# Three row blocks on one ring, a scaling split around a root, and padding moved in TensorE's stream

## The chip, the cores and the metric

One core of one Trainium2 chip runs the whole program. The metric is the device time of one execution in microseconds (us), as a median of several runs; lower is better. A profiled execution lets the engines' instructions be read: TensorE (PE, with its weight loads as PEld), VectorE (DVE), ScalarE (ACT), GpSimd (POOL) and SyncE (SP), which here only issues DMAs.

## The reference

S = 2048 rows of width D = 640, H = 32 heads of size 128, the last W = 512 positions of a key and value cache, and a hidden width of F = 1728, all in fp32.

```
xn  = layernorm(x)                                  # over the last axis, eps 1e-5
q   = (xn @ wq) split into 32 heads of 128
p   = softmax(q k^T / sqrt(128)) over 512 positions # no mask
s   = concat(p v) @ wo                              # 2048 x 640
h   = relu(xn @ w1 + b1) ** 2                       # 2048 x 1728
out = x + s * silu(h @ w2 + b2)
```

## The kernel before

Rows are worked in four tiles of 512 (t = 0 to 3); everything is kept transposed, with the 640 features as 5 chunks of 128 partitions and the 512 rows along the free axis. Each fp32 operand is split into a high and a low part (`hi`, rounded by a ScalarE copy, and `lo`, the rest, by a subtraction on VectorE or GpSimd), and each product is the sum of three TensorE products, hi·hi, hi·lo and lo·hi.

The program has a first part, the MLP of tiles 0 to 2 in 42 steps (14 hidden chunks for each tile, `mlp_step(n)`: `up` of step n, then `down` of step n − 1), and a second, attention in 128 units (two halves, 16 groups of 2 heads, 2 tiles, 2 heads), with the rest of the MLP put in at its end. The order of instructions on each engine is the order in which they are written; in attention, a plan of due times sorts them.

The change lies mostly in `ln_first()`, the layernorm of tile 0, which nothing can run ahead of. Its 512 rows are four blocks of 128 rows, `xn[0]` to `xn[3]`, each 128 x 640. Block 0 comes in two halves, one by SP's DMA queue and one by ScalarE's; block 1 by SP's, block 2 by ScalarE's, block 3 by SP's. Meanwhile TensorE makes 40 transposes of the identity (`pw`) which nobody reads. Then:

- VectorE makes the statistics of a block (two `bn_stats`, one `bn_aggr`), block by block.
- Blocks 0 and 1 share one root: `root(0)` is a ScalarE square root, then a reciprocal on VectorE and a Newton step on GpSimd (`newton(0)`, four small instructions). ScalarE subtracts the mean (`centre`) and multiplies by the root (`scale`), 640 columns at a time; `scale(b)` also has TensorE transpose block b's five chunks (`turn`).
- Blocks 2 and 3 share the second: `root(1)` on ScalarE, between `scale(0)` and `scale(1)`, then the Newton step on VectorE, which also does subtraction and multiplication of both blocks, chunks 0 and 1 of block 2, the same of block 3, then chunks 2 to 4 of each.
- TensorE's transposes of chunk c of all four blocks gather in one PSUM bank, `px0_c`. ScalarE copies it into the high part of `xT`, VectorE makes the low part, and the first `up` starts.

`first_reads` puts the loads of the first weights on SP's queue behind a VectorE memset, so that they come after the x blocks. `ln_load(1)` then puts the next tile's four row blocks on SP's queue; each goes into the buffer of a block of tile 0 and waits until that has been transposed.

`pe.addr_align(BLOCK, slot)` inserts idle slots into TensorE's instruction stream until the next instruction stands at `slot` modulo 256. A matmul or transpose takes two slots (its weight load and itself), a separate wait takes one. In front of the warm-up there is one such alignment, to slot 88; in attention each unit has five (`align`, first at slot 188), which fix where the boundaries of 256 slots fall.

Of the kernel before, what the change touches and what calls it, by code (L numbers as in the profile page):

```python
# [10 lines left out]
AF = mybir.ActivationFunctionType  # L11
# [3 lines left out]
P = 128  # L15
NT = 512
EPS = 1e-5
WARM = 40
BLOCK = 256
FIRST_SLOT = 188  # L20
SLOTS = (0, 11, 22, 33, 42)
LEAD_SLOT = 88


@with_exitstack
def kernel(
# [19 lines left out]
    NB = NT // P  # L46
    DC = D // P
# [3 lines left out]
    LN_AT = {t: (3, 7) if t == LATE else (5, 9) for t in range(1, NTILE)}  # L51
# [12 lines left out]
    chunks = [(f0, min(P, F - f0)) for f0 in range(0, F, P)]  # L64
# [4 lines left out]
    class Ordered:  # L69
# [13 lines left out]
    pe, dve, act, pool, sp = (  # L83
        Ordered(e) for e in (nc.tensor, nc.vector, nc.scalar, nc.gpsimd, nc.sync)
    )
# [49 lines left out]
    def ln_tile(t, b):  # L135
        tag = "stage" if b < 2 else "mr"
        return xp.tile([P, D], F32, tag=tag, name=f"xb{t}_{b}")
# [88 lines left out]
    def ln_first():  # L226
        mv = xp.tile([P, 4, NB], F32, tag="mv", name="mv0")
        sc = xp.tile([P, 3, NB], F32, tag="sc", name="sc0")
        sts = [xp.tile([P, 2, 6], F32, tag="st", name=f"st0_{b}", bufs=4) for b in range(NB)]
        n = NB // 2  # L230
        M, R = ([mv[:, i, n * k : n * k + n] for k in range(2)] for i in range(2))
        VAR, SD, Y = ([sc[:, i, n * k : n * k + n] for k in range(2)] for i in range(3))
        warm = mv[:, 3, :1]
        pool.memset(warm, 1.0)
        eps = mv[:, 3, 1:2]
        dve.memset(eps, EPS)
        hd = D // 2
        xn = [ln_tile(0, b) for b in range(NB)]
        for i, q in enumerate((sp, act)):
            js = slice(i * hd, (i + 1) * hd)  # L240
            q.dma_start(xn[0][:, js], x[:P, js])
        for b in range(1, NB):
            (sp if b % 2 else act).dma_start(xn[b], x[b * P : (b + 1) * P, :])
        act.activation(warm, warm, AF.Sqrt)
        br = xp.tile([P, P], F32, tag="br", name="br", bufs=1)
        dve.memset(br, 0.0)
        BR.append(br)
        pw = psx.tile([P, NT], F32, tag="x", name="pw")
        pe.addr_align(BLOCK, LEAD_SLOT)
        for _ in range(WARM):  # L250
            pe.transpose(pw[:, :P], ident, ident)
        pts = [ps_y.tile([P, NT], F32, tag="py", name=f"px0_{c}") for c in range(DC)]
        xs = [
            xp.tile([P, DC, NT], F32R, tag=f"xT{i}", name=f"xT0_{i}", bufs=1) for i in range(2)
        ]

        def bn(b, i):
            dve.bn_stats(sts[b][:, i, :], xn[b][:, i * hd : (i + 1) * hd])

        def aggr(b):  # L260
            dve.bn_aggr(mv[:, :2, b], sts[b])

        def root(k):
            act.activation(SD[k], R[k], AF.Sqrt, bias=eps)
            dve.tensor_scalar(VAR[k], R[k], EPS, None, op0=ALU.add)

        def newton(k):
            if k == 0:
                pool.tensor_tensor(R[k], Y[k], Y[k], op=ALU.mult)
                pool.tensor_tensor(R[k], R[k], VAR[k], op=ALU.mult)  # L270
                pool.tensor_scalar(R[k], R[k], 0.5, -1.5, op0=ALU.mult, op1=ALU.add)
                pool.tensor_tensor(R[k], R[k], Y[k], op=ALU.mult)
            else:
                dve.scalar_tensor_tensor(R[k], Y[k], -0.5, Y[k], op0=ALU.mult, op1=ALU.mult)
                dve.tensor_tensor(R[k], R[k], VAR[k], op=ALU.mult)
                dve.scalar_tensor_tensor(R[k], R[k], 1.5, Y[k], op0=ALU.add, op1=ALU.mult)

        def centre(b):
            act.activation(xn[b], xn[b], AF.Identity, bias=mv[:, 0, b : b + 1], scale=-1.0)

        def scale(b):
            act.activation(xn[b], xn[b], AF.Identity, scale=R[0][:, b : b + 1])
            turn(b, range(DC))

        def turn(b, cs):
            for c in cs:
                pe.transpose(
                    pts[c][:, b * P : (b + 1) * P], xn[b][:, c * P : (c + 1) * P], ident
                )

        for b in range(n):
            for i in range(2):
                bn(b, i)
            aggr(b)
            if b == 0:
                raws = first_reads(br)
        centre(0)
        root(0)
        centre(1)
        bn(n, 0)  # L300
        dve.reciprocal(Y[0], SD[0])
        newton(0)
        bn(n, 1)
        aggr(n)
        for b in range(n + 1, NB):
            for i in range(2):
                bn(b, i)
            aggr(b)
        scale(0)
        root(1)  # L310
        scale(1)
        split_hi(0, raws[0], 0)
        dve.reciprocal(Y[1], SD[1])
        newton(1)
        for cs in (range(2), range(2, DC)):
            js = slice(cs[0] * P, (cs[-1] + 1) * P)
            for b in range(n, NB):
                m, q = mv[:, 0, b : b + 1], mv[:, 1, b : b + 1]
                dve.tensor_scalar(
                    xn[b][:, js], xn[b][:, js], m, q, op0=ALU.subtract, op1=ALU.mult  # L320
                )
            for c in cs:
                for b in range(n, NB):
                    turn(b, (c,))
        pool.tensor_copy(warm, xn[NB - 1][:, D - 1 :])
        split_lo(0, raws[0], 0, pool)
        for c in range(DC):
            act.activation(xs[0][:, c, :], pts[c], AF.Copy)
            dve.tensor_tensor(xs[1][:, c, :], pts[c], raw(xs[0][:, c, :]), op=ALU.subtract)
        split_hi(1, PRE[1, 0], 0)  # L330
        split_lo(1, PRE[1, 0], 0, pool)
        split_hi(0, raws[1], 1)
        split_lo(0, raws[1], 1, dve)
        return xs

    def spill(t, xs, cs=slice(0, DC)):
        for i in range(2):
            pool.dma_start(xT_d[t][i][:, cs, :], raw(xs[i])[:, cs, :])
# [25 lines left out]
    def split_hi(f, r, k):  # L364
        act.activation(split_parts(f, k)[0], r, AF.Copy)
# [92 lines left out]
    steps = [(t, f) for t in range(LATE) for f in range(FC)]  # L458
    XS, HS, PY, LN = {0: xs_next}, {}, {}, {}

    def gate(t, tiles):
        for d in range(DC):
# [5 lines left out]
            )  # L468
            nc.gpsimd.dma_start(g_d[t][:, d, :], sg)

    def mlp_step(n):
        if n < len(steps):
            t, f = steps[n]
            ln_stats_at, ln_chunk_at = LN_AT[t + 1]
            if t == 0 and f == 1:
                ln_load(1)
            if t == 0 and f == 6:
                LN[1] = ln_root(1)
            if t and f == ln_stats_at - 1:
                ln_load(t + 1)  # L480
            if t and f == ln_stats_at:
                for b in range(NB):
                    ln_block(t + 1, b)
                ln_var(t + 1)
                LN[t + 1] = ln_root(t + 1)
            c = f - ln_chunk_at
            if 0 <= c < DC:
                ln_chunk(t + 1, *LN[t + 1], c)
                XS[t + 1] = LN[t + 1][1]
            if t + 1 == LATE and 0 < c <= DC:  # L490
                spill(t + 1, XS[t + 1], slice(c - 1, c))
            if t == 0 and f > 0:
                split_w(f, 1)
                if f < 8:
                    for k in range(2):
                        load_part(f + 2, k)
            HS[n] = up(t, f, XS[t])
            if t == 0 and 2 <= f < 2 + NB:
                ln_block(1, f - 2)
                if f == NB + 1:  # L500
                    ln_var(1)
            if f == ln_stats_at + 2:
                LN[t + 1] = ln_rows(t + 1, LN[t + 1])
            if t > 0 and f == 1:
                spill(t - 1, XS[t - 1])
            if t == LATE - 1 and f == 3:
                spill(t, XS[t])
        if n > 0:
            t, f = steps[n - 1]
            if f == 0:  # L510
                PY[t] = [
                    ps_y.tile([P, NT], F32, tag="py", name=f"py{t}_{d}") for d in range(DC)
                ]
            down(t, f, HS.pop(n - 1), PY[t])
            if f == FC - 1 and t < LATE - 1:
                gate(
                    t,
                    lambda d: xp.tile(
                        [P, D], F32, tag=("stage", "mr")[d % 2], name=f"sg{t}_{d}"
                    )[:, :NT],  # L520
                )
# [580 lines left out]
    for item in order:  # L1102
        kind, n = item[0], int(item[1:] or 0)
# [125 lines left out]
```

## Time and profile before

| | |
|---|---|
| median of 3 runs | 1960.74 us (1960.03 to 1960.88) |
| profiled execution | 1961.36 us, of which the span from first to last instruction is 1959.6 us |
| instructions in the profile | 28181 |
| TensorE matmuls and transposes | 8616 |

The profile gives, for each instruction, its start and duration, how long its engine was idle before it, and what ended that idle time. Times inside it count from the start of the span. A line such as `2.55 6.51 PE L77 MATMUL pw<-ident 128*128 128x128 f32 x40 [2.55 <-issue]` reads: from 2.55 us on, for 6.51 us, 40 TensorE instructions into `pw`, before which the engine was idle for 2.55 us, ended by nothing that the profile shows. In a windows view each row is a stretch of time, with the busy time of each engine and the number of its instructions in it, the granted TensorE clock, the DMA engines' busy share and what they moved.

### The profile page before, as it was taken

How to read it: one execution, taken by the hardware profiler on the slowest of the kernel's cores; microseconds unless marked ns; L12 is line 12 of the kernel's file. 1: busy time of each engine (PE TensorE's matmuls, PEld its weight loads, DVE VectorE, ACT ScalarE, POOL GpSimd, SP SyncE). 2: the span in 40 equal slices, each digit the busy share in tenths (PEclk: the TensorE clock that was granted, in tenths of full speed). 3: DMA queues.
4: the chain of work that ended last, by engine and by line, in shares of the span. 5: the costliest groups of instructions: out<-in, count | busy, mean ns of one | idle time of the engine just before them, and what ended most of it. 6: DMA issues, size and time to landing. Idle time of an engine off the chain costs nothing.

```text
span 1959.6 us, 28181 instructions
## 1 busy us (share of the span) xinstructions
PE 1951.1 (100%) x8616; PEld 1611.8 (82%) x8616; DVE 1534.8 (78%) x2638; ACT 1187.1 (61%) x2039; POOL 1375.7 (70%) x757
## 2 busy tenths in 40 slices
PE   9999999999999999999999999999999999999998
PEld 7888888888888888888888888888888888888887
DVE  5633337788888888888888878888888888888865
ACT  4432336766666666666666676666666666666643
POOL 2121226888888888888887888888888888888841
PEclk9999999999999999999999999999999999999999
DMA  5330454333333232223335433443333333333353
GB/s 182 94 119 28 183 198 128 98 93 92 92 92 92 92 92 93 92 92 93 92 92 174 145 119 108 114 114 114 113 114 114 114 114 114 98 92 92 85 189 118
DMA packets 127892, 219.13 MB, mean 112 GB/s; under 512 B 23452, under 2 KB 38086, under 8 KB 126470
## 3 DMA queue, kind: packets, MB, share of 16 engines
q1 hardware_dynamic: 124598, 202.43, 34.1%
q0 software_dynamic: 2864, 14.42, 1.8%
q8 instruction: 77, 1.26, 0.2%
q14 instruction: 65, 0.53, 0.1%
q10 hardware_dynamic: 288, 0.49, 0.1%
HBM read 193.41 MB, written 23.87 MB: 111 GB/s over the span
## 4 chain that ended last, share of the span: by engine, by line
PE 98%; DMA 1%; DVE 1%; POOL 0%; ACT 0%; issue 0%; SPq 0%; POOLq 0%; ACTq 0%
PE r L77 22%; PE pq L77 22%; PE o L77 18%; PE s L77 18%; PE ph L425 7%; PE ly L77 2%; PE py L101 2%; PE py L100 2%; PE py L102 2%; PE lu L77 2%; PE eu L77 0%; PE ph L396 0%; POOL pt L77 0%; DMA xb<-in_x_dram 0%; PE py L448 0%; PE py L447 0%
## 5 line engine op out<-in xcount | busy, mean ns | idle before, releaser
L77 POOL TENSOR_TENSOR pt<-e,pt 128x1024 fp32r<-128x1024 f32 x256 | 615.5, 2404 | 115.2 <-ACT pt L77 69.1
L77 PE MATMUL r<-ot,wo 128*128 128x512 f32 x1920 | 496.6, 389 | 0.0
L77 PE MATMUL pq<-ax,wq 128*128 128x512 f32 x1920 | 456.1, 389 | 0.0
L77 PEld LDWEIGHTS pq<-ax,wq 128*128 128x128 f32 x1920 | 360.3, 188 | 75.3 <-DVE q L77 0.4
L77 PEld LDWEIGHTS r<-ot,wo 128*128 128x128 f32 x1920 | 360.4, 188 | 74.9
L77 PE MATMUL o<-pt,wv 128*128 128x512 f32 x1536 | 369.7, 389 | 0.1
L77 PE MATMUL s<-q,wk 128*128 128x512 f32 x1536 | 369.1, 389 | 0.1
L77 DVE TRANSPOSE_TENSOR_REDUCE rdm<-s 128x16 f32<-128x512 f32 x512 | 346.5, 711 | 6.2 <-PE s L77 6.0
L77 ACT ACTIVATE e<-e 128x1024 f32<-128x1024 f32 x256 | 269.8, 1054 | 125.5 <-DVE e L77 82.0
L77 PEld LDWEIGHTS o<-pt,wv 128*128 128x128 f32 x1536 | 288.1, 188 | 60.9 <-POOL pt L77 1.2
L77 PEld LDWEIGHTS s<-q,wk 128*128 128x128 f32 x1536 | 288.1, 188 | 60.5 <-DVE e L77 0.7
L77 DVE TENSOR_TENSOR e<-s,bm 128x512 f32<-128x512 f32 x512 | 312.2, 664 | 7.6 <-DMA bm<-m_d 7.1
L77 POOL TENSOR_TENSOR su<-e,e 128x1024 f32<-128x1024 f32 x128 | 309.1, 2415 | 0.0
L77 ACT ACTIVATE pt<-e 128x1024 fp32r<-128x1024 f32 x256 | 272.0, 1063 | 6.9
L77 DVE TENSOR_TENSOR acc<-r,acc 128x512 f32<-128x512 f32 x300 | 203.4, 678 | 12.9 <-PE r L77 12.6
L77 ACT ACTIVATE rdm<-rdm 32x64 f32<-32x64 f32 x384 | 97.8, 255 | 181.5 <-DVE rdm L77 178.4
L77 DVE TRANSPOSE_TENSOR_REDUCE rds<-su 128x32 f32<-128x1024 f32 x128 | 158.3, 1237 | 0.3 <-POOL su L77 0.3
L77 DVE TENSOR_TENSOR ot<-o,ot 128x512 fp32r<-128x512 f32 x128 | 88.5, 691 | 86.1 <-ACT ot L77 86.1
L77 ACT ACTIVATE q<-pq 128x512 fp32r<-128x512 f32 x128 | 76.7, 600 | 111.5 <-PE pq L77 111.4
L425 PE MATMUL ph<-xT,w1s 128*128 128x512 f32 x585 | 139.5, 390 | 0.0
L425 PEld LDWEIGHTS ph<-xT,w1s 128*128 128x128 f32 x585 | 109.5, 188 | 23.5 <-DVE xT L77 0.9
L77 ACT ACTIVATE rds<-rds 32x32 f32<-32x32 f32 x384 | 89.7, 234 | 63.0 <-DVE rds L77 59.7
(137 smaller groups left out, 1940.9 us busy)
## 6 DMA issues: line engine op xcount, KB each, us to landing
bm<-m_d SPq DMA_DIRECT2D x128, 256.0 KB, 3.2
bs<-s_d SPq DMA_DIRECT2D x128, 256.0 KB, 4.0
qr<-in_wq_dram SPq DMA_DIRECT2D x64, 320.0 KB, 4.5
or<-in_wo_dram SPq DMA_DIRECT2D x64, 320.0 KB, 4.7
kr<-in_kT_dram SPq DMA_DIRECT2D x64, 256.0 KB, 4.3
vr<-in_v_dram SPq DMA_DIRECT2D x64, 256.0 KB, 4.4
xT_d<-xT POOLq DMA_DIRECT2D x6, 1280.0 KB, 8.0
ax<-xT_d SPq DMA_DIRECT2D x4, 1280.0 KB, 10.6
```

What stands on the lines that cost most here:

```text
L77: ins = method(*args, **kwargs)
L100: nc.tensor.matmul(ps, ah, bh, start=first and i == 0, stop=False)
L101: nc.tensor.matmul(ps, ah, bl, start=False, stop=False)
L102: nc.tensor.matmul(ps, al, bh, start=False, stop=last and i == n - 1)
L425: nc.tensor.matmul(ph, w1s[f][i][:, c, :], xs[j][:, c, :], start=k == 0, stop=k == len(order) - 1,)
```

## The change

- Blocks 1, 2 and 3 all go through SP's queue, one behind another. ScalarE's queue carries half of block 0 only.
- `scale(0)` becomes two ScalarE instructions, chunks 0 to 2 (384 columns) before `root(1)` and chunks 3 and 4 (256 columns) behind it. `scale` does not transpose any more: block 0's five transposes are written after its second piece, and block 1's go chunk by chunk with those of blocks 2 and 3.
- The warm-up has 38 transposes instead of 40, and no alignment in front.
- In steps 19 to 27 (the second tile's from its chunk 5 on) an alignment is put between `up` and `down`; its slot is worked out from the instructions ahead of it, plus 5 more at each step.

```
-WARM = 40
+WARM = 38
-LEAD_SLOT = 88
+LEAD_SLOTS, LEAD_PADS, LEAD_STEPS = 177, 5, range(19, 28)
...
         for b in range(1, NB):
-            (sp if b % 2 else act).dma_start(xn[b], x[b * P : (b + 1) * P, :])
+            sp.dma_start(xn[b], x[b * P : (b + 1) * P, :])
...
-        pe.addr_align(BLOCK, LEAD_SLOT)
...
-        def scale(b):
-            act.activation(xn[b], xn[b], AF.Identity, scale=R[0][:, b : b + 1])
-            turn(b, range(DC))
+        def scale(b, cs):
+            js = slice(cs[0] * P, (cs[-1] + 1) * P)
+            act.activation(xn[b][:, js], xn[b][:, js], AF.Identity, scale=R[0][:, b : b + 1])
...
-        scale(0)
+        scale(0, range(3))
         root(1)
-        scale(1)
+        scale(0, range(3, DC))
+        turn(0, range(DC))
+        scale(1, range(DC))
...
             for c in cs:
-                for b in range(n, NB):
+                for b in range(1, NB):
                     turn(b, (c,))
...
+    def lead_slot(n):
+        ups = sum(2 * (2 if chunks[steps[k][1]][1] < P else 3) * DC for k in range(n + 1))
+        downs = sum(2 * (2 if chunks[steps[k][1]][1] < P else 3) * DC for k in range(n - 1))
+        turns = 2 * sum(1 for k in range(n + 1) if steps[k][1] == LN_AT[steps[k][0] + 1][0] + 2)
+        return (LEAD_SLOTS + ups + downs + turns + LEAD_PADS * (n - LEAD_STEPS[0])) % BLOCK
...
+            if n in LEAD_STEPS:
+                pe.addr_align(BLOCK, lead_slot(n))
```

## The prediction

> **What bounds the kernel now.** I read the page first: busy time of each engine, then the chain that ended last.
>
> ```profile
> span 1959.6 us, 28181 instructions
> PE 1951.1 (100%) x8616; PEld 1611.8 (82%) x8616; DVE 1534.8 (78%) x2638; ACT 1187.1 (61%) x2039; POOL 1375.7 (70%) x757
> PE 98%; DMA 1%; DVE 1%; POOL 0%; ACT 0%; issue 0%; SPq 0%; POOLq 0%; ACTq 0%
> ```
>
> TensorE carries 98% of the chain. The windows view, cut where the work changes, shows where the other 2% can be:
>
> ```profile
> core 0: us, PE busy (x) PEld busy (x) DVE busy (x) ACT busy (x) POOL busy (x), PEclk, DMA share, GB/s
> 2.50:6.50 4.00, 3.95 (x19) 3.98 (x20) 2.01 (x7) 1.49 (x3) 0.00 (x0) 1.00 0.88 316
> 6.50:9.10 2.60, 2.56 (x23) 2.32 (x21) 2.46 (x10) 1.61 (x3) 0.78 (x4) 1.00 0.92 273
> 9.10:12.40 3.30, 2.81 (x19) 2.12 (x20) 2.52 (x10) 2.67 (x6) 0.47 (x2) 1.00 1.02 336
> 20.40:315.80 295.40, 295.36 (x1303) 243.33 (x1304) 121.83 (x207) 107.10 (x165) 64.51 (x79) 1.00 0.37 128
> 315.80:1950.00 1634.20, 1633.94 (x7203) 1350.99 (x7202) 1396.20 (x2390) 1066.94 (x1853) 1305.31 (x664) 1.00 0.36 107
> ```
>
> From 20.4 us on, TensorE starts a matmul every 295.40/1303 = 0.2267 us, and in attention every 1634.20/7203 = 0.2269 us: it never runs dry. No part of the change touches the number of matmuls there (the 8616 become 8614, both from the warm-up), so it can move the end only by moving the moment at which this stream starts to run without gaps, or by putting a gap into it. That leaves the first 20 us. There the chain, in order of time, reads:
>
> ```profile
> 1.19 4.34 DMA xb<-in_x_dram
> 5.56 0.90 DVE st L77 x2
> 6.48 0.22 DVE mv L77
> 7.29 0.08 DVE sc L77
> 8.28 0.21 POOL mv L77
> 8.51 0.83 ACT xb L77
> 9.34 0.20 ACT sc L77
> 9.56 0.18 DVE sc L77
> 10.35 1.52 DVE xb L77 x4
> 11.92 0.77 PE px L77 x5
> 12.68 2.81 PE ph L425 x10
> 15.60 4.56 PE ph L425 x20
> 23.93 3.40 PE ph L425 x15
> ```
>
> So the start is one chain: block 1 of x lands; its statistics; the first root and Newton step (VectorE, then GpSimd); block 0's scaling on ScalarE; the second root, which stands behind that scaling on ScalarE; the second Newton step; the scaling of blocks 2 and 3; transposes; first matmuls. TensorE's own warm-up is not on it.
>
> **Part 1: blocks 1 to 3 on SP's ring.** The timeline of VectorE and TensorE in that stretch:
>
> ```profile
> 2.55 6.51 PE L77 MATMUL pw<-ident 128*128 128x128 f32 x40 [2.55 <-issue]
> 9.39 3.29 PE L77 MATMUL px<-ident,xb 128*128 128x128 f32 x20 [0.33 <-ACT xb L77]
> 3.54 0.89 DVE L77 BATCH_NORM_STATS2 st<-xb 128x6 f32<-128x320 f32 x2 [2.50 <-DMA xb<-in_x_dram]
> 4.62 0.06 DVE L77 MEMSET w1r<- 128x1 f32 x1
> 5.56 0.89 DVE L77 BATCH_NORM_STATS2 st<-xb 128x6 f32<-128x320 f32 x2 [0.88 <-DMA xb<-in_x_dram]
> 6.80 0.49 DVE L77 BATCH_NORM_STATS2 st<-xb 128x6 f32<-128x320 f32 x1
> 7.91 0.83 DVE L77 BATCH_NORM_STATS2 st<-xb 128x6 f32<-128x320 f32 x2
> 8.78 0.21 DVE L77 BATCH_NORM_AGGREGATE mv<-st 128x2 f32<-128x12 f32 x1
> ```
>
> VectorE waits 0.88 us for block 1 and never for blocks 2 and 3. Now block 1 (SP) and block 2 (ScalarE's ring) travel at once and each takes about half of the bandwidth; in one ring block 1 goes ahead. The rate:
>
> ```profile
> 3.30:5.60 2.30, 2.30 (x13) 2.30 (x12) 1.14 (x5) 0.83 (x1) 0.00 (x0) 1.00 0.97 367
> 7.00:8.00 1.00, 1.00 (x11) 1.00 (x10) 0.97 (x5) 0.74 (x2) 0.39 (x2) 1.00 1.07 382
> ```
>
> Both rings together moved 367 GB/s at 3.3 to 5.6 us; SP's ring, by then alone, 382 GB/s at 7 to 8 us, so one ring is enough. A block is 320 KB = 0.328 MB, 0.89 us at 367 GB/s. Block 0 was there when its statistics began, at 3.54. Estimate: block 1 at 3.54 + 0.89 = 4.43, block 2 at 5.3, block 3 at 6.2. VectorE is free at 4.68, so block 1's wait goes wholly: the statistics start at 4.70 instead of 5.56, **0.86 us earlier**. The bounds are 0 (block 1 lands as late as before) and 0.88. What is late next? Block 2 is then wanted at 6.80 − 0.86 = 5.94 and block 3 at 7.05, both after the estimates. SP issues one transfer more before the weights, but the weights' first issue waits for the memset at 4.62 anyway. So the first root, block 0's scaling and the last aggregate all come 0.86 earlier: scaling at 7.65, last aggregate ended at 8.13.
>
> **Part 2: block 0's scaling split around the second root.** ScalarE's rows:
>
> ```profile
> 6.73 0.29 ACT L77 ACTIVATE sc<-mv 128x2 f32<-128x2 f32 x1 [1.19 <-DVE mv L77]
> 9.24 0.28 ACT L77 ACTIVATE sc<-mv 128x2 f32<-128x2 f32 x1
> 10.15 0.72 ACT L77 ACTIVATE w1s<-w1r 128x640 fp32r<-128x640 f32 x1
> 11.50 2.56 ACT L77 ACTIVATE xT<-px 128x512 fp32r<-128x512 f32 x5 [0.63 <-PE px L77]
> 27.95 0.46 ACT L77 ACTIVATE w1s<-w1r 128x320 fp32r<-128x320 f32 x1
> ```
>
> The first root started 0.04 us after its aggregate (6.48 + 0.21 = 6.69, root at 6.73). The second could have started at 8.99 + 0.04 = 9.03, but stood behind a 640-column scaling and came at 9.24. With 384 columns ahead of it (about 0.53 us, between the 0.46 of 320 columns and the 0.72 to 0.83 of 640) the scaling ends at 8.18, and as the next instruction started 0.10 before the end of the last one (9.24 against 9.34), ScalarE is free at 8.08; the root is wanted at 8.13 + 0.04 = 8.17. It starts at 8.17 instead of 9.24: **1.07 earlier**, 0.21 of it from the split. The price is one ScalarE instruction more, about 0.2 us of fixed time (0.46 + 0.46 against 0.72). It lies after the root: the second piece at 8.36, block 1's scaling at 8.65 to 9.47, the weight split at 9.37 to 10.1. The first copy to xT is wanted at 11.50 − 1.07 = 10.43, so 0.3 us of cover are left.
>
> **Part 3: order of the transposes.** Block 1's five transposes move from in front of blocks 2 and 3 to between their chunks. Chunk 0 needs block 3's first half, 1.07 earlier than before (about 10.07); block 1 has been ready since 9.47, so the first copy loses nothing. At the end three transposes per chunk stand where two stood: two more of 0.11 us (2.60/23), so the first matmul starts at 12.44 − 1.07 + 0.22 = 11.59. That is hidden: the second matmul waits for VectorE's first low part of xT, which comes 1.07 earlier at about 11.8, and so do the next four. Block 1's buffer is now freed with its last chunk, at about 11.7, and the load of the next tile's rows into it waits for that on SP, with two more such loads and the next weights behind it. Those two wait for blocks 2 and 3, whose last chunks come at the same time, so SP loses nothing against them; the rows themselves are wanted by the statistics at
>
> ```profile
> 30.48 0.88 DVE L77 BATCH_NORM_STATS2 st<-xb 128x6 f32<-128x320 f32 x2
> ```
>
> some 19 us later. Everything behind (biases, first hidden block, the short wait at 20.0) hangs on that chain and moves along.
>
> **Part 4: 38 warm-up transposes and no alignment in front.** TensorE's first start, at 2.55, was released by "issue": it was stepping over padding. Without padding it starts when the identity is there, at 1.32 (below), so about 1.4. In the windows 2.5 to 6.5 a transpose took 0.21 us, from 6.5 on 0.113: the array runs at half rate for about 4 us. Starting at 1.4, 38 transposes end at about 7.5 (19 slow, 19 fast), at worst 9.5 if all were slow. Block 0's first chunks are ready at 8.2, block 1 at 9.47, and nothing before 10.07 is on the chain: worth 0 either way.
>
> ```profile
> 1.03 0.29 POOL masks.py:199 TENSOR_SCALAR_AFFINE_SELECT ident<-ident 128x128 f32<-128x128 f32 x1
> ```
>
> **Part 5: padding in steps 19 to 27.** Counted from the program, the nine alignments insert five slots each (the first one slot if the program starts at slot 50 of its page) and the total stays the same, so attention's alignment is unchanged. Attention already carries some 20 slots of padding in each unit of 54 matmuls, and it runs at 0.2269 us a matmul against 3.40/15 = 0.2267 where there is none: at most 0.0002 × 54/20 = 0.0005 us a slot. Forty-five slots: 0 to 0.03 us; I take 0. The page boundaries of the stream shift by some 20 matmuls until step 27; no wait of TensorE in the trace of before stands at one, so I price that at 0 too.
>
> **Sum.** 0.86 + 0.21 = 1.07 us earlier at the second root, nothing lost or gained behind it: −1.07. The profiled execution took 1961.36 for its span of 1959.6; it would take 1960.3. It lies 0.62 above the median of the runs, 1960.74 (1960.03 to 1960.88), so the forecast is 1960.74 − 1.07 = **1959.7**, 0.05% faster. A measurement of this kernel tells about 0.2% (3.9 us) from no change, so this counts as none.
>
> **Rivals.** (a) Block 1 lands no earlier, since the transfers' start and not the sharing delays it: only the split counts, 0.21 us, 1960.5. Against it: the 0.97 share of busy DMA while it waited. 8%. (b) One ring does not keep its rate for rows of x: at half of 367 GB/s a block takes 1.79 us, and blocks 1 to 3 at 5.3, 7.1, 8.9 would make block 3 late by 8.9 − 7.91 = 1.0, less the split's 0.21: 1960.74 + 0.8 = 1961.5. It decides once block 3 lands after 7.91. Against it: 382 GB/s above. 4%. (c) The clock.
>
> ```profile
> 1958.00:1959.60 1.60, 0.00 (x0) 0.00 (x0) 0.00 (x0) 0.00 (x0) 0.00 (x0) 0.81 0.00 1
> ```
>
> The granted clock does fall when TensorE has nothing to do (x0), at the very end. It will now have little to do from 7.5 to 10: some six transposes. If that counted as idle, half rate for as long as at the start, 4 us, would cost at most 2 us: 1959.7 + 2.0 = 1961.7. The Trainium skill, "TensorE: Matmul & The Clock Gate", Part 4, says that transposes don't count as TensorE work and don't raise the clock. By that rule the danger is larger, and every first matmul would be slow before and after; the trace disagrees, as the rate doubled at about 6.5 us with nothing but transposes run. 5%. (d) The slower side: the padding. The first alignment asks for slot 255 where the stream stands at 204 plus the program's start slot, modulo 256. If the program starts one slot past 51, the alignment inserts up to 255 slots at once. The price: before, 88 less the start slot, some 37 slots, took at least the 2.55 − 1.4 = 1.15 us by which the warm-up came late and at most the whole 2.55, so 0.031 to 0.069 us a slot and 7.9 to 17.6 us for 255. I take the lower, as TensorE works off its queue meanwhile: 1959.7 + 7.9 = 1967.6. For it: nothing in the trace names the start slot. Against: with a start past 51 fewer than 37 slots would have to fill that time. 6%.
>
> **Numbers.** The forecast has 77%, and its own range is 1959.0 to 1960.4: the runs' spread of 0.85 around it, and the gain's uncertainty of 0.2. Rivals (a) to (c), 17%, reach to 1961.7; (a) and half of the others lie below 1961.0. Range 1958.9 to 1961.0; left out are (d), half of (b) and (c), and the tails. Slower by over 0.2% is (d), 0.06; faster would need 3.9 us, which the first 20 us don't hold: 0.02; same 0.92.
>
> **What the profile after would show.** Right: no wait of VectorE for the DMA of x after block 0, statistics of block 1 at about 4.7, the second root at about 8.2, the first copy to xT at 10.4, the stream without gaps from about 19.3. Wrong: a VectorE wait for x at block 2 or 3; first matmuls at half rate; a gap near step 19 (about 138 us); or a second root still behind ScalarE.

## The result, and the profile after

The changed kernel takes 1975.4 us (median of 6 runs, 1974.31 to 1976.69), the one before 1960.66 us (median of 6, 1960.03 to 1961.04). The ratio is 1.0076, with a 95% interval of 1.0063 to 1.0089: slower by 14.7 us where 1.1 us less was forecast. The profiled execution took 1974.31 us for its span of 1972.5.

The page of the changed kernel, its first lines, its chain, and the queue that fetches instructions (packets, MB, share):

```profile
span 1972.5 us, 28438 instructions
PE 1952.1 (99%) x8614; PEld 1613.5 (82%) x8614; DVE 1536.7 (78%) x2638; ACT 1187.0 (60%) x2040; POOL 1374.7 (70%) x757
...
q8 instruction: 78, 1.28, 0.2%
...
PE 98%; issue 1%; ACT 1%; DVE 0%; DMA 0%; POOL 0%; POOLq 0%
```

TensorE's busy time is 1 us more and its span 12.9 us longer. In the chain "issue" went from 0% to 1%: time in which the engine waited for nothing that the profile shows. And there are 257 instructions more, although the change was to leave the sum of idle slots about as it was: 260 are idle slots, counted below, one is ScalarE's second piece of block 0's scaling, and four are gone with the two transposes left out of the warm-up.

The timeline of the changed kernel, in the first 20 us and around step 19:

```profile
1.37 7.11 PE L77 MATMUL pw<-ident 128*128 128x128 f32 x38 [1.37 <-POOL mv L77]
4.61 0.49 DVE L77 BATCH_NORM_STATS2 st<-xb 128x6 f32<-128x320 f32 x1
5.77 0.29 ACT L77 ACTIVATE sc<-mv 128x2 f32<-128x2 f32 x1 [0.22 <-DVE mv L77]
5.88 0.49 DVE L77 BATCH_NORM_STATS2 st<-xb 128x6 f32<-128x320 f32 x1
6.99 0.83 DVE L77 BATCH_NORM_STATS2 st<-xb 128x6 f32<-128x320 f32 x2
7.58 0.62 ACT L77 ACTIVATE xb<-xb,mv 128x384 f32<-128x384 f32 x1 [0.80 <-POOL mv L77]
8.11 0.29 ACT L77 ACTIVATE sc<-mv 128x2 f32<-128x2 f32 x1
8.30 1.21 ACT L77 ACTIVATE xb<-xb,mv 128x256 f32<-128x256 f32 x2
10.38 2.56 ACT L77 ACTIVATE xT<-px 128x512 fp32r<-128x512 f32 x5 [0.24 <-PE px L77]
11.53 2.84 PE L426 MATMUL ph<-xT,w1s 128*128 128x512 f32 x10
19.32 0.50 PE L101 MATMUL py<-h,w2s 128*128 128x512 f32 x1
...
133.94 3.56 PE L426 MATMUL ph<-xT,w1s 128*128 128x512 f32 x15
151.00 0.77 PE L100 MATMUL py<-h,w2s 128*128 128x512 f32 x1 [13.50 <-issue]
151.56 0.63 PE L101 MATMUL py<-h,w2s 128*128 128x512 f32 x1
151.99 0.63 PE L102 MATMUL py<-h,w2s 128*128 128x512 f32 x1
153.70 0.46 PE L100 MATMUL py<-h,w2s 128*128 128x512 f32 x1
153.99 0.39 PE L101 MATMUL py<-h,w2s 128*128 128x512 f32 x1
```

The head went as forecast: the second root, at 9.24 before, is at 8.11, and the second matmul of the first `down` (`py` at line 101) is at 19.32. Then, between the `up` and the `down` of step 19, where the first of the new alignments stands, TensorE is idle for 13.50 us, and the matmuls behind that come 0.43 us apart (151.56 to 151.99) until 153.7.

The windows around it (columns as in the prediction):

```profile
core 0: us, PE busy (x) PEld busy (x) DVE busy (x) ACT busy (x) POOL busy (x), PEclk, DMA share, GB/s
130.00:137.00 7.00, 7.00 (x33) 5.79 (x32) 2.50 (x7) 1.32 (x2) 1.04 (x1) 1.00 0.02 4
137.00:151.00 14.00, 0.50 (x4) 0.11 (x2) 3.61 (x14) 2.69 (x4) 1.04 (x1) 0.61 0.13 37
151.00:154.00 3.00, 3.00 (x8) 2.37 (x9) 0.00 (x0) 0.00 (x0) 0.00 (x0) 0.53 0.02 5
154.00:160.00 6.00, 6.00 (x28) 4.96 (x27) 0.00 (x0) 0.51 (x1) 0.00 (x0) 1.00 0.00 0
```

In the 3 us after the stop the granted clock is 0.53 and eight matmuls are counted, 0.43 us apart; in the 6 us after that it is 1.00 and 28 are counted, 0.23 us apart. So there are two losses at this place: the stop, and a slow stretch behind it. In the waits view of the whole stream from 20.4 us on, a single wait of TensorE stands out:

```profile
PE py L100 <- issue: 13.5, 1, 13.5
```

The views leave idle slots out, but the trace records each as an instruction of TensorE's sequencer. Counted from those records (not a view):

```
            all slots   the one long run of slots               apart (middle)
before      2528        23 slots, 0.83 to 2.48 us (warm-up)     71 ns
after       2788        242 slots, 133.28 to 150.93 us          71 ns
            (the eight alignments of steps 20 to 27: 5 slots each)
```

Twenty-three slots lead from the program's start to slot 88, so the program starts at slot 88 − 23 = 65 of its page of 256. The first new alignment then finds the stream at 204 + 65 = 269, that is 13, when it asks for 255, and 242 slots are inserted. From first to last that takes 17.65 us, on average 0.073 us a slot. TensorE still had work queued until 137.34, 4.06 us after the first slot; the rest, some 13.6 us, is the stop.

The difference of the two profiled executions adds up so, by the starts of three matmuls in each trace: up to the last one ahead of the stop −1.12 us (138.24 before, 137.11 after); from there past the slow stretch +15.08, of which 13.66 are the stop and 1.42 the slow matmuls; in attention −1.02, where the profiled execution of before has four short waits of TensorE of 1.35 us together. The prediction read that stream as never running dry and passed over these waits; that they are mostly gone in the profile after was not traced to the change. Together 12.94, and the spans differ by 12.9. The medians differ by 14.7, the 15.1 less some 1.1 of the head being 14.0; the remaining 0.7 us was not traced to anything.

### The profile page after: what moved, and what is told of

It is laid out like the page before. It is cut to its first block, busy times and chain, and to the rows that moved or that the text cites. A ratio compares the mean times of both kernels' runs of the same rounds, so it can differ in the third digit from the quotient of the medians.

```text
span 1972.5 us, 28438 instructions
## 1 busy us (share of the span) xinstructions
PE 1952.1 (99%) x8614; PEld 1613.5 (82%) x8614; DVE 1536.7 (78%) x2638; ACT 1187.0 (60%) x2040; POOL 1374.7 (70%) x757
## 4 chain that ended last, share of the span: by engine, by line
PE 98%; issue 1%; ACT 1%; DVE 0%; DMA 0%; POOL 0%; POOLq 0%
PE pq L77 22%; PE r L77 22%; PE o L77 18%; PE s L77 18%; PE ph L426 6%; PE ly L77 2%; PE py L101 2%; PE py L100 2%; PE py L102 2%; PE lu L77 2%; PE eu L77 1%; PE ph L397 0%; PE py L448 0%; PE py L449 0%; DMA xb<-in_x_dram 0%
## 5 line engine op out<-in xcount | busy, mean ns | idle before, releaser
L77 DVE TENSOR_TENSOR acc<-r,acc 128x512 f32<-128x512 f32 x300 | 203.4, 678 | 13.0 <-PE r L77 12.9
L384 POOL TENSOR_TENSOR r<-r 128x512 f32<-128x512 f32 (+1 forms) x28 | 29.1, 1038 | 152.5 <-ACT r L438 139.0
```

What stands on the lines that cost most here:

```text
L77: ins = method(*args, **kwargs)
L384: g.tensor_tensor(r, r, r, op=ALU.mult)
```

## The experiments

The theory: the idle slots cost 0.073 us each on TensorE's sequencer, hidden as long as matmuls are queued (4.06 us of them here), and all of the loss comes from 242 standing in one run. Rival 1: every added slot costs time wherever it stands. Rival 2: the one more page of instructions to fetch (q8: 78 packets instead of 77) stops the engine. Rival 3: something in the new head delays the stream later on. The first four kernels tell these apart.

**The same kernel with slots that fit the start.** Runs of 1 and 3 slots instead of 242 and 5:

```
-LEAD_SLOTS, LEAD_PADS, LEAD_STEPS = 177, 5, range(19, 28)
+LEAD_SLOTS, LEAD_PADS, LEAD_STEPS = 192, 3, range(19, 28)
```

> The whole change with its padding fitted to the stream: base 192 instead of 177 and 3 slots a step instead of 5, so that counted from the program's start at slot 65 the nine alignments insert 1 and then 3 slots each and attention's first one 4; all other alignments as before. Theory (the first alignment in step 19 found the stream 14 slots past its slot and filled up 242 at once): no gap at step 19, 77 instruction pages, the head's 1.1 us gained: 1959.6, ratio 0.9994. Rival 1 (padding in the lead costs by the slot, about 14/286 = 0.05 us each): 25 slots of 0.05 = 1.3 us, nothing left of the gain: 1960.8. Rival 2 (the gap is a page fetch that comes late wherever an alignment meets a page boundary): a gap stays, 1970 or more.

Measured: 1959.68 us, ratio 0.9994 (0.9985 to 1.0003). Its page and its window over step 19:

```profile
span 1958.0 us, 28182 instructions
...
q8 instruction: 77, 1.26, 0.2%
```

```profile
130.00:160.00 30.00, 30.00 (x134) 24.75 (x134) 8.02 (x24) 7.35 (x11) 4.69 (x5) 1.00 0.12 36
```

256 instructions fewer, no stop (30.00 of 30.00 us busy), clock 1.00. The new head is in this kernel and nothing is late behind it: rival 3 falls.

**The head only**, with the alignment in front and 40 transposes as before, and no slots in the steps:

```
-WARM = 38
+WARM = 40
...
+        pe.addr_align(BLOCK, LEAD_SLOT)        # LEAD_SLOT = 88, in front of the warm-up
...
-            if n in LEAD_STEPS:
-                pe.addr_align(BLOCK, lead_slot(n))
```

> The x blocks on one ring, the split scaling and the new order of transposes, with the 40 warm-up transposes and the alignment in front as before and no padding in the steps. Theory: the chain from block 1 gains 0.86 us and the split 0.21, the warm-up ends at about 9.1, after block 0's first chunks (8.2) but before block 1's scaling (9.5), so it costs nothing: 1959.6, ratio 0.9994. Rival (the head's gain hangs on the warm-up's earlier start): the transposes of block 0 end at 9.7 and push block 1's, 0.2 us lost: 1959.8 to 1960.0.

Measured: 1959.98 us, 0.9995 (0.9986 to 1.0004). In its profile the second root is at 8.34, and the transposes of block 0 start only at 9.42, behind the late warm-up. The first `up` starts at 11.76 all the same, 3.42 us behind the second root, as in the changed kernel (11.53 − 8.11): the late warm-up costs nothing there. The median is 0.3 us above the kernel with fitting slots, too little for the runs to tell; this profile also has a wait of TensorE of 0.6 us at 225.6, taken up below with the head's two edits.

**The padding only**, on the head of before:

```
-WARM = 40
+WARM = 38
...
-        pe.addr_align(BLOCK, LEAD_SLOT)
...
+            if n in LEAD_STEPS:
+                pe.addr_align(BLOCK, lead_slot(n))
```

> The kernel before with the padding of the change alone: 38 warm-up transposes, no alignment in front, the nine alignments in steps 19 to 27 with the change's slots. Theory: the whole loss is there: one run of 242 slots, TensorE stopped 13.7 us at step 19 and slow for eight matmuls behind it: 1960.7 + 15.8 = 1976.5, ratio 1.008. Rival (part of the loss comes from the head, by transfers that collide later): less than 1974.

Measured: 1976.1 us, 1.0078 (1.0064 to 1.0092). Its window over the stop:

```profile
138.65:152.40 13.75, 0.39 (x2) 0.00 (x0) 3.50 (x14) 2.69 (x4) 1.04 (x1) 0.61 0.12 36
```

The loss is whole on the head of before: 15.3 us by the medians, of which the trace shows 13.64 as the stop and 1.43 as slow matmuls behind it.

**As many slots, spread.** The nine alignments insert 31 slots each, 279, and attention's first one 6, together 285 as in the changed kernel (242 + 8 × 5 + 3):

```
-LEAD_SLOTS, LEAD_PADS, LEAD_STEPS = 177, 5, range(19, 28)
+LEAD_SLOTS, LEAD_PADS, LEAD_STEPS = 222, 31, range(19, 28)
```

> The whole change with the same 279 slots of padding in steps 19 to 27 spread evenly, 31 in each of the nine steps (base 222, 31 a step), and 6 at attention's first alignment; as many slots and pages in all as in the changed kernel. Theory (a run costs only what goes beyond TensorE's queued work, about 4 us, since the queue stood 3.8 us ahead when the run of 242 began): a run of 31 x 0.071 = 2.2 us is hidden and the lead is made up within a step of 6.8 us: 1959.6. Rival 1 (by the slot): 279 x 0.05 = 14 us, 1974. Middle: the lead is not made up in one step, each run beyond the first costs up to 2.2 us: up to 1977.

Measured: 1959.52 us, 0.9994 (0.9985 to 1.0003). Its page and windows:

```profile
span 1957.7 us, 28438 instructions
...
q8 instruction: 78, 1.28, 0.2%
```

```profile
130.00:160.00 30.00, 30.00 (x135) 24.73 (x134) 7.78 (x23) 7.35 (x11) 5.05 (x5) 1.00 0.13 36
160.00:205.00 45.00, 45.00 (x200) 37.28 (x199) 17.16 (x26) 15.31 (x23) 7.64 (x10) 1.00 0.08 24
```

The same 28438 instructions and the same 78 packets as the changed kernel, and nothing lost. This settles it against rivals 1 and 2: neither the number of slots nor the page costs time, only how many stand in one run. The Trainium skill, "Runtime: NRT & Kernel Launch", section "Instruction fetch mechanics", says that crossing into the next 16 KiB of instructions is mostly hidden; this run agrees, with 0 us seen for one page more.

Next, the size of a run was varied: 48 in one run, 110 in one, and three of 93 to 96.

**A run of 110**, then eight of 21:

```
-LEAD_SLOTS, LEAD_PADS, LEAD_STEPS = 177, 5, range(19, 28)
+LEAD_SLOTS, LEAD_PADS, LEAD_STEPS = 45, 21, range(19, 28)
```

> The whole change with one run of 110 slots in step 19, 21 in each of the eight others and 7 at attention's first alignment. Theory: 110 x 0.073 - 4.0 = 4.0 us of stop in step 19, the runs of 21 hidden: 1959.6 + 4.0 = 1963.6; with a lowered clock behind it up to 1.6 more, 1965.2. Rival (a stop needs a full page of padding): 1959.6.

Measured: 1965.72 us, 1.0024 (1.0015 to 1.0034). Its windows:

```profile
137.60:141.57 3.97, 0.08 (x1) 0.03 (x1) 3.19 (x13) 2.69 (x4) 1.04 (x1) 1.00 0.38 114
142.10:145.50 3.40, 3.40 (x9) 2.63 (x8) 0.00 (x0) 0.00 (x0) 0.00 (x0) 0.50 0.00 0
145.50:150.00 4.50, 4.50 (x21) 3.70 (x20) 0.00 (x0) 0.00 (x0) 0.00 (x0) 1.00 0.00 0
```

The stop is 4.05 us from the trace's starts (110 × 0.073 − 4.06 = 3.97). Then eight matmuls start in 3.40 us at a clock of 0.50 (the row also counts one that was already running), where fifteen would at the usual 0.227: with the edges of the stretch 1.7 us lost. The two make 5.8, and with the head's gain of 1.1 the kernel should stand 4.7 above the one before; it stands 4.9 above.

**Three runs of 93, 96 and 96**, at steps 19, 23 and 27:

```
-LEAD_SLOTS, LEAD_PADS, LEAD_STEPS = 177, 5, range(19, 28)
+LEAD_SLOTS, LEAD_PADS, LEAD_STEPS = 28, 24, range(19, 28, 4)
```

> The whole change with the same 285 slots in steps 19 to 27 as three runs of 93, 96 and 96, in steps 19, 23 and 27. Theory (a run costs its length by 0.073 us less about 4.0 us of queued work): 93 x 0.073 - 4.0 = 2.8 us, 96 x 0.073 - 4.0 = 3.0 us twice, 8.8 us in all, and TensorE stands still too short to be slowed: 1959.6 + 8.8 = 1968.4. If each stop also lowers the clock for as long as after the stop of 13.7 us (1.6 us lost): 1973. Rival (only the one run of 242 ends at a page boundary and stalls there): no loss, 1959.6.

Measured: 1973.63 us, 1.0064 (1.005 to 1.0077): 5 us above the theory's 1968.4, and near the 1973 of a lowered clock behind each stop. Its windows, cut every 3.41 us (the reason stands below), two or more for each stop:

```profile
137.33:140.75 3.42, 0.75 (x4) 0.35 (x3) 2.81 (x11) 2.69 (x4) 1.04 (x1) 1.00 0.47 152
140.75:144.16 3.41, 3.41 (x9) 2.62 (x9) 0.84 (x3) 0.00 (x0) 0.00 (x0) 0.50 0.00 0
168.05:171.47 3.42, 1.70 (x8) 1.08 (x6) 0.69 (x1) 0.81 (x2) 0.86 (x1) 1.00 0.28 75
171.47:174.88 3.41, 2.37 (x10) 1.99 (x11) 1.99 (x3) 1.11 (x2) 0.17 (x1) 1.00 0.01 2
198.77:202.19 3.42, 1.22 (x6) 0.68 (x4) 0.43 (x1) 0.95 (x2) 1.04 (x1) 1.00 0.00 0
202.19:205.60 3.41, 2.72 (x7) 2.17 (x8) 0.69 (x1) 0.36 (x1) 0.00 (x0) 0.50 0.02 5
205.60:209.02 3.42, 3.42 (x10) 2.65 (x9) 0.00 (x0) 0.00 (x0) 0.00 (x0) 0.50 0.00 0
209.02:212.43 3.41, 3.41 (x16) 2.81 (x15) 0.00 (x0) 0.00 (x0) 0.00 (x0) 1.00 0.00 0
```

From the trace's starts the stops are 2.83, 2.93 and 3.05 us, 8.81 together, where the queue's cover taken off each run gives 285 × 0.073 − 3 × 4.06 = 8.6. In all 13.6 us are lost at the three places; the other 4.8 lie behind the stops: 1.7 behind the first and 3.0 behind the third, at a clock of 0.50, and only 0.1, at 1.00, behind the second, which was no shorter than the first. So the length of the stop alone does not decide whether the clock falls. The Trainium skill, "TensorE: Matmul & The Clock Gate", section "Why this matters for your kernels", puts the limit at gaps of about 3 us; of these stops around it the shortest and the longest were followed by the low clock, and the one between was not.

What tells them apart in the traces is where the stop falls. A trace also records when the granted clock changed, and in each of the twelve profiles these moments lie whole multiples of 3.413 us apart: here 40, 1, 17 and 2 of them lie between one change and the next, in the changed kernel 39 (7.03 to 140.15) and 4 (to 153.81). So the clock changes on a grid, and where the grid lies in the program differs from one execution to the next. Over all twelve profiles the clock fell at the end of every stretch of this grid in which TensorE was busy for 1.22 us or less, and of none with 1.55 or more; it rose at the end of every stretch with 2.81 or more, and of none with 2.72 or less. The first and the third stop leave 0.75 and 1.22 us of work in one stretch. The second is cut by the grid at 171.47 and leaves 1.70 and 2.37. Behind the third stop the stretch from 202.19 holds 2.72 us, so the low clock lasts two stretches instead of one. These bounds were read off the traces afterwards; no run was made to test them.

**A run of 48**, then eight of 29:

```
-LEAD_SLOTS, LEAD_PADS, LEAD_STEPS = 177, 5, range(19, 28)
+LEAD_SLOTS, LEAD_PADS, LEAD_STEPS = 239, 29, range(19, 28)
```

> The whole change with a first run of 48 slots in step 19, 29 in each of the eight other steps and 5 at attention's first alignment, 285 in all. Theory (a run is free up to the 4.0 us that TensorE has queued): 48 x 0.073 = 3.5 us, hidden, no stop at step 19: 1959.6, as with 31 slots a step. Rival (the cost grows with the first run from zero: 110 slots cost 6.0 us, so 48 cost 2.6): 1962.2.

Measured: 1959.38 us, 0.9995 (0.9986 to 1.0004). 48 slots are 3.5 us, less than the 4.06 queued, and its window shows no stop (no run between 48 and 93 slots was tried):

```profile
130.00:160.00 30.00, 30.00 (x135) 24.73 (x134) 7.82 (x24) 7.35 (x11) 4.89 (x5) 1.00 0.12 36
```

**No padding in the steps**, so that the 29 slots that are then missing stand in one run at attention's first alignment:

```
-LEAD_SLOTS, LEAD_PADS, LEAD_STEPS = 177, 5, range(19, 28)
+LEAD_SLOTS, LEAD_PADS, LEAD_STEPS = 177, 5, ()
```

> The whole change without any alignment in the steps: 38 warm-up transposes, none in front, and the 29 slots that attention's first alignment then needs in one run there. Theory: 29 x 0.073 = 2.1 us, hidden behind queued matmuls if TensorE has some 4 us queued there too: 1959.6; the padding in the steps is then worth nothing. Rival (at attention's first unit the queue is short, since its matmuls wait for the first scores' operands): up to 2.1 us lost, 1961.7.

Measured: 1959.34 us (11 runs, 1959.06 to 1959.64), 0.9993 (0.9984 to 1.0003). Its window where the 29 slots stand:

```profile
290.00:302.00 12.00, 12.00 (x55) 9.93 (x54) 6.83 (x11) 5.58 (x8) 3.04 (x9) 1.00 0.72 273
```

So padding in the steps is worth nothing here: without it the kernel stands 1.2 us below the one before by the medians. Its interval takes in no change, but all of its 11 runs lie below the lowest of the 21 runs of before beside it (1959.97).

**The head's two edits by themselves**, on the kernel before. One ring only:

```
-            (sp if b % 2 else act).dma_start(xn[b], x[b * P : (b + 1) * P, :])
+            sp.dma_start(xn[b], x[b * P : (b + 1) * P, :])
```

> The kernel before with blocks 1 to 3 on SP's ring and nothing else changed. Theory: block 1's statistics start at 4.6 to 4.7 instead of 5.56, everything behind comes 0.86 us earlier, the second root still stands behind the whole scaling of block 0: 1960.8 - 0.86 = 1959.9, span 0.86 shorter. Rival (the split alone brings the gain): 1960.8.

Measured: 1960.48 us, 0.9998 (0.9989 to 1.0007), 0.37 below the 1960.85 of before beside it. Its timeline:

```profile
4.94 0.89 DVE L77 BATCH_NORM_STATS2 st<-xb 128x6 f32<-128x320 f32 x2 [0.29 <-DMA xb<-in_x_dram]
6.60 0.49 DVE L77 BATCH_NORM_STATS2 st<-xb 128x6 f32<-128x320 f32 x1 [0.32 <-DMA xb<-in_x_dram]
8.30 0.83 ACT L77 ACTIVATE xb<-xb,mv 128x640 f32<-128x640 f32 x1 [1.18 <-POOL mv L77]
9.04 0.28 ACT L77 ACTIVATE sc<-mv 128x2 f32<-128x2 f32 x1
...
221.54 0.89 DVE L77 BATCH_NORM_STATS2 st<-xb 128x6 f32<-128x320 f32 x2 [3.85 <-DMA xb<-in_x_dram]
226.32 0.50 PE L447 MATMUL py<-h,w2s 128*128 128x512 f32 x1 [0.45 <-DVE h L387]
```

The split only, with its order of transposes and blocks 1 to 3 on two rings:

```
...
-        scale(0)
+        scale(0, range(3))
         root(1)
-        scale(1)
+        scale(0, range(3, DC))
+        turn(0, range(DC))
+        scale(1, range(DC))
```

> The kernel before with the split scaling of block 0 and the new order of transposes alone, blocks on two rings as before. Theory: the second root starts at 9.03 instead of 9.24: 0.21 us, 1960.6. Rival (order of the transposes costs as much): 1960.8.

Measured: 1960.49 us, 0.9998 (0.9989 to 1.0007), 0.36 below. Its timeline:

```profile
5.25 0.89 DVE L77 BATCH_NORM_STATS2 st<-xb 128x6 f32<-128x320 f32 x2 [0.44 <-DMA xb<-in_x_dram]
8.71 0.29 ACT L77 ACTIVATE sc<-mv 128x2 f32<-128x2 f32 x1
```

On one ring block 1 was waited for 0.29 us instead of 0.88 and block 2 for 0.32 instead of 0, and without the split the second root stood behind block 0's scaling (8.30 + 0.83 = 9.13, root at 9.04). With the split it stands behind nothing: it comes 0.53 us earlier than before (8.71 against 9.24), 0.32 of that because the last aggregate ended earlier (8.67 against 8.99) and 0.21 by the split, the size forecast for it. On one ring the last aggregate ended only 0.20 earlier than before, not 0.86, as block 2 came late. Both edits act where the prediction put them; of their sizes the medians say only that each is a few tenths of a microsecond, as the intervals of ±1.8 us hold them all.

Part of the gain is lost again later in these two profiles. VectorE stands waiting for rows of the last tile (until 221.54 on one ring), what it does next comes late, and a `down` of TensorE waits for it: 0.61 us on one ring and 0.90 with the split, by the starts. The 0.6 us of the head alone is the same wait. The profiles of before, of the changed kernel and of the one with fitting slots have none there, so it doesn't come with the new head each time; whether it comes with some of the kernels or only in some executions, one profile of each can't tell.

## Why the prediction was wrong, step by step

**Part 5 failed, at its premise.** The prediction let the alignments insert five slots each "(the first one slot if the program starts at slot 50 of its page)" and priced them at 0. The start was taken, not read. It is 65, past the 51 from which the alignment wraps. The trace of before held it, as 23 records of idle slots ahead of the warm-up; the prediction worked from a view that leaves these records out and saw "issue" instead. Its second premise, the price of a slot from attention's stream (at most 0.0005 us), is a price under cover: there few slots stand in one run. The spread kernel shows that price right where it holds, 256 slots more for nothing.

**Rival (d) came true, at 6%.** Its mechanism was this one, with its place (step 19, about 138 us) and its point of decision. Its chance was set low by the argument that with a start past 51 "fewer than 37 slots would have to fill that time", which excludes nothing: 23 slots at 71 ns are the 1.65 us from 0.83 to 2.48. With nothing in the views that fixes the start, the starts that wrap were as open as those that don't. Its price had three terms mis-sized:

- the slots: 242, not 255, at 0.073 us, not 0.031 to 0.069 (37 slots had been assumed where 23 stood): 17.65 us;
- the cover: the lower end, 7.9, was taken "as TensorE works off its queue meanwhile", without asking how much that is; it is 4.06 us, which leaves 13.6, against 13.66 measured;
- the clock behind the stop, 1.42 us, was in no term.

So it would have been 1959.7 + 15.1 = 1974.8, against 1975.4 measured, where the prediction gave 1967.6.

**Parts 1 and 2 were right, in the profile after and as a mean.** Block 1's statistics: forecast 4.70, measured 4.61; second root 8.17, measured 8.11; gain at the second matmul of `down` 1.07, measured 20.44 − 19.32 = 1.12. But when the rows land differs from one execution to the next: the kernel that fits the slots waited 0.72 us for block 2 (second root 8.76), which the estimate "block 2 at 5.3" excludes. In the eight profiles with the whole new head the second root is at 8.11 to 8.76, on average 8.41, so the close match of 8.11 is partly luck; in the two with the old head it is at 9.24 and 9.69. In medians the head is worth 0.8 to 1.3 us in the five kernels that have it without a long run of slots. Rivals (a) and (b) did not come: block 1 did land earlier, and block 3 was never waited for.

**Part 3 was right**: the first `up` at 11.53 (11.59 forecast), the first copy to `xT` at 10.38 (10.43).

**Part 4 was right in its worth, not in its times.** The warm-up starts at 1.37, as worked out, but ends at 8.48 (7.5 was forecast, 9.5 at worst), so in this profile TensorE never had the idle stretch from 7.5 to 10 on which rival (c) hung. The kernel with fitting slots had one of 1.60 us there, and its first `up` was as fast (10 matmuls in 2.86 us, 2.84 in the changed kernel), so rival (c) did not come. The transposes went from 0.21 to 0.11 us apart at about 7.0 us, where the granted clock rose, with nothing but transposes ahead, as in before; this is against the rule of the Trainium skill that the prediction weighed ("TensorE: Matmul & The Clock Gate", Part 4).

**The range and the chances**: all of the range hung on the first 20 us, in which the change was well read, and next to none on the one edit whose input, the start slot, was unknown. Among the signs that would show it wrong it named "a gap near step 19 (about 138 us)", and that is what the profile shows.

## What to carry to other kernels

An edit that pads to an address depends on where the stream stands when it gets there: read that from the trace's count of idle slots in the kernel before, and where it can't be read, give the wrap its full share of the chance. Padding is free as long as one run of it is shorter than the work queued on the engine (here 48 slots, 3.5 us, against 4.06 us) and costs its full time beyond, with a stretch at half clock behind it in most of the stops seen here, so spread it or leave it out. When a page's count of instructions rises by more than the edit adds, look for idle slots before anything else.

## What the runs showed of the hardware that was not expected

- An idle slot holds TensorE's sequencer for 0.071 to 0.073 us; beside it the queued matmuls go on, one every 0.227 us, until the queue is empty after 4.06 us, about 18 matmuls of 128x512.
- The granted clock changed only at whole multiples of 3.413 us from one change to the next, in all twelve profiles. So it matters where a stop falls as well as how long it is: at half clock matmuls are 0.43 us apart instead of 0.227, and that went on for some 3.6 us behind a stop of 2.83 us, 6.1 behind one of 3.05, 2.8 behind the one of 13.66, and not at all behind one of 2.93.
- Block 1's statistics started between 4.49 and 5.07 us on one ring and between 5.25 and 5.84 on two, in the profiled executions of otherwise equal loads.
